# Steps of five engines issued in the order of a written timetable, in place of a list scheduler's order

## The chip, the cores and the metric

The kernel runs on one core of a Trainium2 chip. The metric is the device time of one execution in microseconds, the median of several runs. A core has five engines that work side by side: TensorE (PE, matmuls; PEld is its weight load), VectorE (DVE), ScalarE (ACT), GpSimd (POOL) and SyncE (SP, which here issues DMA transfers). Each takes its instructions strictly in the order in which the program wrote them; semaphores make an instruction wait for its inputs and for its buffer.

## The reference, cut to what matters

Two parts follow each other. The first is a gated recurrence with a complex decay for 4 batches, 8 heads, 768 time steps and 48 channels per head:

```python
mag = np.sqrt(a_re * a_re + a_im * a_im)
scale = np.minimum(mag, 0.999) / (mag + 1e-06)
a_re_n, a_im_n = (a_re * scale, a_im * scale)
for t in range(S):
    new_re = ar * S_re - ai * S_im
    new_im = ar * S_im + ai * S_re
    S_re, S_im = (new_re + kv, new_im)            # kv = outer(k[t], v[t])
    y[:, :, t] = einsum('bhd,bhde->bhe', q[:, :, t], S_re)
```

The second takes y as 3072 tokens of 384 features: `(sigmoid(x @ w_gate) * (x @ w_val)) @ w_out`, with 1536 hidden features. The result is 3072 x 384 in float32.

## The kernel before

**Slabs and groups.** The 768 time steps of a batch are cut into 6 chunks of 128, which gives 24 slabs of 128 tokens by 384 features (8 heads of 48). Slabs are taken in groups, `SIZES = [2, 3, 3, 3, 3, 3, 3, 3, 1]`. In logarithms the product of decays is a running sum, so a chunk becomes a masked attention (scores between q and k, each scaled by its decay and turned by its angle) plus a state that goes from chunk to chunk.

**The steps.** The program is a list of small steps, each on one engine, named by kind and slab m (or group g):

- *Loads, on SP:* `consts` (six constants), `la` (a_re and a_im of a slab), `lq` (k, q and v of a slab). The weights `wg`, `wv`, `wo` are loaded from POOL's queue in nine parts.
- *Phase A, for a whole group:* `sq` (squares, ACT, line 333); `add` and `min` on POOL (342, 350) make the capped squared size; `lna`, `lnm`, `inv` on ACT (358, 365, 371) take logarithms and a reciprocal; `r` on POOL (382) is the ratio of the parts; `cl` on PE (389) sums the logarithms over time; `ee` on ACT (396, 398) gives the decays as exp of plus and minus half the sum. `scr` and `rbe` on SP (405, 413) send the last row of the decays to DRAM and bring it back as columns.
- *Phase B:* `atan` on ACT (449).
- *Phase C, for each slab:* `ct` on PE (463, and 466 for what was carried from earlier chunks) sums the angles, `run` on POOL (479, 482) carries them on, `r16` on DVE (490) and `nid` on PE (498) take off whole turns, `cs` on ACT (506 to 509) takes cosine and sine. `v16` on POOL (433) casts v, `qke` on POOL (441) multiplies q and k by the decays, `ks` and `qs` on DVE (518) turn them.
- *Attention of a slab:* `tp` (PE, 548 and 549: 16 transposes in two halves), `qkT` (DVE, 556), `sc` (PE, 564), `mst` (DVE, 571: mask), `u` (DVE, 585 and 588: the state, decayed), `x16` (POOL, 598), `kv` (PE, 608), `P` (DVE, 618, 621: the new state), `y` (PE, 634, 636), `y16` (ACT, 646), `xp` (PE, 655), `xt` (DVE, 662).
- *The second part, for a group:* for each of 12 blocks of 128 hidden features, `pg` and `pv` (PE, 679, three matmuls each over all tokens of the group), `tanh` (ACT, 694), `p` (DVE, 701, the product); then for each slab `po` (PE, 717, 12 matmuls in three steps), `ot` (ACT, 727) and `st` (SP, 734, the store).

**Tables of ACT.** Phase A, B and C each need another table of functions (`SETS`); tanh is in those of B and C. Changing it is an instruction of its own (line 769, or the line of the instruction for which the compiler had to add it).

**Buffers.** Each tile kind has a fixed number of buffers: two for `a2` (the group's a), one for `sq`, six for q and k, four for v, and in PSUM four tiles for attention (`gen`) and four for the second part (`moe`).

**What sets the order.** `Plan.order` is a list scheduler. Each step has an engine, a cost, a due time and a list of steps that it must follow. The scheduler keeps a clock for each engine, takes the earliest start that any ready step could have, and picks, on that engine, the step with the earliest due time:

```python
t, _, k, eng = min((c for c in cand if c[3] == best[1]
                    and c[0] <= best[0] + SLACK),
                   key=lambda c: (c[1], c[0]))
```

Due times come from `RATE` (9.21 us a slab) and leads and lags (`LEAD`, `MOE_LAG`). A phase of the next group is entered by the rules in `may_enter`. The order found is written out once; the tile framework adds the semaphore waits.

Of the kernel before, what the change touches and what calls it, by code (L numbers as in the profile page):

```python
# [26 lines left out]
SIZES = [2, 3, 3, 3, 3, 3, 3, 3, 1]  # L27
RATE = 9.21
LEAD = {'la': 87.6, 'lq': -0.9, 'p0': 39.8, 'pa': 40.0, 'pb': 17.2}
MOE_LAG = -5.7  # L30
WGV_DUE, WOU_DUE, WGV_AFTER = -41.6, 45.5, 0
SLACK = 0.05
TAIL = {"pe": 0.21, "dve": 0.14, "act": 0.17, "pool": 0.11, "sp": 0.0}


class Plan:
# [6 lines left out]

    def __init__(self):
        self.steps, self.bufs, self.caps = {}, {}, {}

    def buf(self, name, tag, make):
        self.bufs[name] = [tag, make, 0]

    def add(self, key, eng, cost, due, emit, after=(), new=(), use=(),  # L50
            phase=None, load=0.0):
        for n in (*new, *use):
            self.bufs[n][2] += 1
        self.steps[key] = (eng, cost, due, emit, tuple(after), tuple(new),
                           (*new, *use), phase, load)

    def order(self, phases, may_enter):
        steps, bufs = self.steps, self.bufs
        users, waits = {}, {}
        for key, st in steps.items():  # L60
            waits[key] = len(st[4])
            for d in st[4]:
                users.setdefault(d, []).append(key)
        left = {n: b[2] for n, b in bufs.items()}
        freed = dict.fromkeys(bufs, 0.0)
        taken = {t: [] for t in self.caps}
        free = dict.fromkeys(ENGINES, 0.0)
        dma = 0.0
        done, placed, avail = {}, [], {}
        ready = {k for k in steps if not waits[k]}  # L70
        for k in ready:
            avail[k] = 0.0
        ph = 0
        while ready:
            while ph + 1 < len(phases) and may_enter(
                    phases[ph + 1], done, free["act"]):
                ph += 1
                if phases[ph][1]:
                    free["act"] += 1.3
            best = None  # L80
            cand = []
            for k in ready:
                eng, _, due, _, _, new, _, want, _ = steps[k]
                if want is not None and phases[ph][0] not in want:
                    continue
                t = max(avail[k], free[eng])
                for n in new:
                    tag = bufs[n][0]
                    old = taken[tag]
                    if len(old) >= self.caps[tag]:  # L90
                        m = old[-self.caps[tag]]
                        if left[m]:
                            t = None
                            break
                        t = max(t, freed[m])
                if t is None:
                    continue
                cand.append((t, due, k, eng))
                if best is None or t < best[0]:
                    best = t, eng  # L100
            if best is None:
                why = []
                for k in ready:
                    eng, _, due, _, _, new, _, want, _ = steps[k]
                    why.append((k, "phase" if want is not None and phases[ph][0] not in want else [ (n, taken[bufs[n][0]][-self.caps[bufs[n][0]]], ) for n in new if len(taken[bufs[n][0]]) >= self.caps[bufs[n][0]] and left[taken[bufs[n][0]][-self.caps[bufs[n][0]]]]]))
                raise RuntimeError(f"no step can be placed: {why} {phases[ph]}")
            t, _, k, eng = min((c for c in cand if c[3] == best[1]
                                and c[0] <= best[0] + SLACK),
                               key=lambda c: (c[1], c[0]))
            _, cost, _, _, _, new, uses, _, load = steps[k]  # L110
            ready.discard(k)
            free[eng] = t + cost
            end = t + cost + TAIL[eng]
            if load:
                dma = max(dma, t + cost) + load
                end = dma + 2.0
            for n in new:
                taken[bufs[n][0]].append(n)
            for n in uses:
                left[n] -= 1  # L120
                freed[n] = max(freed[n], end)
            done[k] = end
            placed.append(k)
            for u in users.get(k, ()):
                waits[u] -= 1
                avail[u] = max(avail.get(u, 0.0), end)
                if not waits[u]:
                    ready.add(u)
        assert len(placed) == len(steps), (len(placed), len(steps))
        self.length = max(done.values())  # L130
        return placed

    def emit(self, order):
        tiles = {}
        for key in order:
            st = self.steps[key]
            for n in st[5]:
                tiles[n] = self.bufs[n][1](n)
            st[3](tiles)


def act_us(n):
    return 0.06 + n * 0.00083


def dve_us(n, fast=False):
    return 0.065 + n / (1920.0 if fast else 960.0)


def pool_us(n, two=False):  # L150
    return 0.15 + n * 0.00215 if two else 0.05 + n * 0.0012


def pe_us(n, passes=1):
    return max(0.025, passes * n / 2400.0 + 0.002)
# [3 lines left out]
def kernel(  # L159
# [12 lines left out]
    nc = tc.nc  # L172
# [11 lines left out]
    NG = len(SIZES)  # L184
    NSLOT = 6
# [4 lines left out]
    nid_d = nc.inline_tensor(-eye, name="glk_nid")  # L190
    wl_d = nc.inline_tensor((tri - 0.5).astype(np.float32), name="glk_wl")
    wt_d = nc.inline_tensor((tri / TWO_PI).astype(np.float32), name="glk_wt")
    on_d = nc.inline_tensor(
        np.full((L, L), 1.0 / TWO_PI, np.float32), name="glk_on")
    msk_d = nc.inline_tensor(tri.astype(np.float32), name="glk_msk")

    def pool(name, bufs, **kw):
        return ctx.enter_context(tc.tile_pool(name=name, bufs=bufs, **kw))

# [6 lines left out]
    def kind(tag, bufs, shape, dt, where=work):  # L206
        plan.caps[tag] = bufs

        def declare(*ids, shape=shape, dt=dt):
            first = ids if isinstance(ids[0], str) else (tag, *ids)  # L210
            name = "_".join(map(str, first))
            plan.buf(name, tag, lambda name: where.tile(
                shape, dt, name=name, tag=tag, bufs=bufs))
            return name

        return declare
# [23 lines left out]
    plan.caps["slot"] = NSLOT  # L240

    def cload(shape, dt, src, name):
        t = const.tile(shape, dt, name=name)
        consts.append((t, src))
        return t

    consts = []
    wl_t = cload([L, L], F32, wl_d, "wl_t")
    wt_t = cload([L, L], F32, wt_d, "wt_t")
    on_t = cload([L, L], F32, on_d, "on_t")  # L250
    idn_t = cload([L, L], F16, idn_d, "idn_t")
    nid_t = cload([L, L], F16, nid_d, "nid_t")
    msk_t = cload([L, L], F32, msk_d, "msk_t")
# [18 lines left out]

    def heads(ap):
        return ap.rearrange("p (h d) -> p h d", d=D)

    def add(key, eng, cost, due, emit, **kw):
        plan.add(key, eng, cost, due, emit, **kw)
        return key


    def e_consts(T):
        for t, src in consts:
            nc.sync.dma_start(t, src.ap())

    add("consts", "sp", 2.7, -90.0, e_consts, load=1.8)
    gv_keys, ou_keys = [], []
    for i, f in enumerate(range(0, DFF, 512)):
        for nm, dst, src in (("wg", wg16, moe_w_gate), ("wv", wv16, moe_w_val)):
            def e(T, dst=dst, src=src, f=f):
# [4 lines left out]
            after = gv_keys[-1:] or [("min", WGV_AFTER)]  # L294
            gv_keys.append(add((nm, i), "pool", 0.77, WGV_DUE, e,
                               after=after, load=2.2))
    for i, j in enumerate(range(0, NFB, 4)):
        def e(T, j=j):
# [5 lines left out]
        ou_keys.append(add(("wo", i), "pool", 0.77, WOU_DUE, e,  # L304
                           after=(ou_keys or gv_keys)[-1:], load=2.2))
# [6 lines left out]
    last_run, last_P = {}, {}  # L312
    TANH_IN = [(x, g) for x in "BC" for g in range(NG)]
    for g, n in enumerate(SIZES):
        m0 = FIRST[g]
        at0 = m0 * RATE
        A, SQ, LM = t_a2(g), t_sq(g), t_lm(g)
        XT, PT = t_xt(g), t_p(g)
        phA, phB, phC = ("A", g), ("B", g), ("C", g)
        for s in range(n):  # L320
# [3 lines left out]
            def e(T, A=A, s=s, b=b, c=c):  # L324
                dma_in(T[A][:, 0, s], a_re, b, c)
                dma_in(T[A][:, 1, s], a_im, b, c)

            add(("la", m), "sp", 0.95, at0 - LEAD["la"] + s, e,
                after=[("la", m - 1)] if m else [],
                new=[A] if s == 0 else [], use=[A] if s else [], load=2.3)  # L330

        def e(T, A=A, SQ=SQ, n=n):
            nc.scalar.activation(out=T[SQ][:, :, :n], in_=T[A][:, :, :n],  # L333
                                 func=FT.Square)

        add(("sq", g), "act", act_us(2 * n * HD), at0 - LEAD["p0"], e,
            after=[("la", m0 + n - 1)], new=[SQ], use=[A])
        for s in range(n):
            m = m0 + s

            def e(T, SQ=SQ, LM=LM, s=s):
                nc.gpsimd.tensor_tensor(out=T[LM][:, s], in0=T[SQ][:, 0, s],  # L342
                                        in1=T[SQ][:, 1, s], op=ALU.add)
# [397 lines left out]
    for g in range(NG):  # L741
        if g:
            phases.append((("A", g), True))
# [57 lines left out]
```

## Time and profile before

| | |
|---|---|
| median of 3 runs | 331.49 us (330.77 to 332.27) |
| the profiled execution | 330.96 us |
| its span, first to last instruction | 328.5 us |
| mean granted clock of TensorE | 0.963 |
| busy: PE, DVE, ACT, POOL | 262.5, 206.5, 211.9, 166.1 us |
| table loads on ACT | 33 of 1.283 us |
| data moved by DMA | 32.68 MB, of that 3.54 from POOL's queue (weights) |

Busy times of an engine are the time in which at least one of its instructions runs. Matmuls are pipelined: each takes longer from start to end than the next one waits to start, so distances between starts tell what PE can do. A row of the timeline or chain gives start, duration, engine, line and tiles; "x4" says how many instructions were merged. A bracket at the end tells how long the engine stood idle before it and what released it. Group rows give busy time in total, the mean of one in ns, and then the idle time ahead. PEclk is the granted clock of TensorE as a share of full speed.

### The profile page before, as it was taken

The numbers are of one execution on the slowest core, as the hardware profiler recorded it, in microseconds if no ns is written. First come the engines' busy times: TensorE is split into PE (matmuls) and PEld (weight loads), VectorE is DVE, ScalarE is ACT, GpSimd is POOL, SyncE is SP. The second block draws the span as 40 slices with busy tenths as digits, with TensorE's granted clock in tenths as the row PEclk, the third lists the DMA queues.
The fourth block names the chain that finished last, engine by engine and source line by source line (L and its number), as shares of the span: only waits on it lengthen the run. The fifth ranks groups of instructions, "written<-read, shape, count | busy, mean of one in ns | idle before, by whom it ended". The sixth has DMA issues, their size and how long they took to land.

```text
span 328.5 us, 6196 instructions
## 1 busy us (share of the span) xinstructions
PE 262.5 (80%) x2256; PEld 169.7 (52%) x2256; DVE 206.5 (63%) x373; ACT 211.9 (65%) x354; POOL 166.1 (51%) x177
## 2 busy tenths in 40 slices
PE   0035685857978799898969989989999898999995
PEld 0012552535545455465646555656666565666564
DVE  2002930399699679287755696689567949891522
ACT  0356438666877987896389848867995358543433
POOL 0187275867997877687117961945485104000000
PEclk9997757799999999999998999999999999999999
DMA  6998995997999588581886048736120011002011
GB/s 124 188 182 128 189 178 85 138 196 108 160 123 218 76 129 160 123 145 11 148 166 113 1 82 154 153 54 118 50 26 2 0 50 28 0 2 73 2 48 48
DMA packets 152381, 32.68 MB, mean 99 GB/s; under 512 B 144904, under 2 KB 152352, under 8 KB 152352
## 3 DMA queue, kind: packets, MB, share of 16 engines
q1 hardware_dynamic: 148368, 28.76, 51.2%
q0 software_dynamic: 3984, 3.54, 7.6%
q8 instruction: 17, 0.28, 0.4%
q14 instruction: 12, 0.10, 0.1%
HBM read 31.07 MB, written 4.76 MB: 109 GB/s over the span
## 4 chain that ended last, share of the span: by engine, by line
PE 42%; ACT 20%; DVE 18%; issue 8%; SPq 4%; DMA 4%; POOL 3%; DVEq 0%; ACTq 0%; POOLq 0%
PE o L717 12%; PE g L679 8%; PE v L679 7%; PE cl L389 5%; ACT L769 5%; DVE qkT L556 4%; DVE p L701 3%; DVE qst L518 3%; DVE kst L518 3%; SPq L309 3%; PE ct L463 2%; ACT g L694 2%; ACT sq L333 2%; ACT a L449 2%; POOL lm L342 2%
## 5 line engine op out<-in xcount | busy, mean ns | idle before, releaser
L694 ACT ACTIVATE g<-g 128x384 f16<-128x384 f32 (+2 forms) x108 | 48.2, 456 | 55.4 <-PE g L679 53.5
L701 DVE SCALAR_TENSOR_TENSOR p<-g,v 128x384 f16<-128x384 f16 (+2 forms) x108 | 53.7, 504 | 23.2 <-PE v L679 15.7
L679 PE MATMUL g<-xt,wg 128*128 128x384 f16 (+2 forms) x324 | 65.5, 312 | 3.0 <-DVE xt L662 1.5
L679 PE MATMUL v<-xt,wv 128*128 128x384 f16 (+2 forms) x324 | 65.5, 312 | 0.9 <-DVE p L701 0.9
L717 PE MATMUL o<-wo,p 128*128 128x384 f16 x288 | 52.0, 326 | 0.0
L389 PE MATMUL cl<-lm,wl_t 128*128 128x384 f32 x48 | 22.7, 607 | 27.8 <-ACT lm L365 24.9
L441 POOL TENSOR_TENSOR qk<-qk,ee 128x768 f32<-128x768 f32 x24 | 43.3, 1813 | 2.0 <-ACT ee L398 2.0
L490 DVE TENSOR_SCALAR r<-ct 128x384 f16<-128x384 f32 x24 | 13.2, 552 | 43.9 <-PE ct L463 25.9
L679 PEld LDWEIGHTS <-wg 128*128 128x128 f16 x324 | 29.5, 99 | 20.5 <-issue 8.0
L679 PEld LDWEIGHTS <-wv 128*128 128x128 f16 x324 | 28.7, 99 | 17.0 <-issue 5.8
L518 DVE TENSOR_TENSOR kst<-qk,cs 128x768 f16<-128x768 f32 x24 | 26.1, 1089 | 17.6 <-ACT cs L509 17.5
L556 DVE COPY qkT<-tp 128x1024 f16<-128x1024 f16 x48 | 32.6, 683 | 6.9 <-PE tp L549 6.6
L598 POOL CAST x<-u 128x384 f16<-128x384 f32 x20 | 14.1, 707 | 44.4 <-DVE u L588 38.4
L717 PEld LDWEIGHTS <-p 128*128 128x128 f16 x288 | 27.1, 98 | 18.2 <-issue 2.1
L571 DVE TENSOR_TENSOR mst<-sc,msk_t 128x512 f16<-128x512 f32 x48 | 32.6, 684 | 5.5 <-PE sc L564 5.4
L342 POOL TENSOR_TENSOR lm<-sq 128x384 f32<-128x384 f32 x24 | 28.1, 1170 | 13.7 <-ACT sq L333 12.3
L769 ACT ACT_TABLE_LOAD x27 | 34.6, 1283 | 0.5
L382 POOL TENSOR_TENSOR a<-a 128x384 f32<-128x384 f32 x24 | 23.6, 1008 | 22.0 <-ACT a L371 19.5
L463 PE MATMUL ct<-a,wt_t 128*128 128x384 f32 x48 | 22.1, 544 | 8.9 <-ACT a L449 8.9
L549 PE MATMUL tp<-idn_t,qst 128*128 128x128 f16 x192 | 26.5, 221 | 3.2 <-DVE qst L518 3.2
L389 PEld LDWEIGHTS cl<-lm,wl_t 128*128 128x128 f32 x48 | 10.4, 235 | 34.9 <-ACT lm L365 28.9
L548 PE MATMUL tp<-idn_t,kst 128*128 128x128 f16 x192 | 27.0, 221 | 0.8 <-DVE P L618 0.4
(52 smaller groups left out, 462.6 us busy)
## 6 DMA issues: line engine op xcount, KB each, us to landing
a<-in_a_re_dram SPq DMA_DIRECT2D x24, 192.0 KB, 3.9
a<-in_a_im_dram SPq DMA_DIRECT2D x24, 192.0 KB
qk<-in_k_dram SPq DMA_DIRECT2D x24, 192.0 KB, 4.9
qk<-in_q_dram SPq DMA_DIRECT2D x24, 192.0 KB, 4.8
v<-in_v_dram SPq DMA_DIRECT2D x24, 192.0 KB, 4.1
out_dram<-ot SPq DMA_DIRECT2D x24, 192.0 KB, 1.9
wg<-in_moe_w_gate_dram POOLq DMA_DIRECT2D x3, 384.0 KB, 5.7
wv<-in_moe_w_val_dram POOLq DMA_DIRECT2D x3, 384.0 KB, 6.4
```

The source lines that it names most:

```text
L342: nc.gpsimd.tensor_tensor(out=T[LM][:, s], in0=T[SQ][:, 0, s], in1=T[SQ][:, 1, s], op=ALU.add)
L389: nc.tensor.matmul(T[CL][:, :HD], wl_t, T[LM][:, s], start=True, stop=True)
L441: nc.gpsimd.tensor_tensor(out=T[QK], in0=T[QK], in1=T[EE], op=ALU.mult)
L463: nc.tensor.matmul(ct, wt_t, T[A][:, 1, s], start=True, stop=False, skip_group_check=True)
L518: nc.vector.tensor_tensor(out=T[SL][i].rearrange("p h (r x) -> p h r x", r=2)[:, :, :, 0:D], in0=heads(T[QK][:, i]).unsqueeze(2) .broadcas ...
L556: nc.vector.tensor_copy(out=T[QT], in_=T[TP])
L571: nc.vector.tensor_tensor(out=T[MS], in0=T[SC], in1=msk_t.unsqueeze(1).broadcast_to([L, 4, L]), op=ALU.mult)
L679: nc.tensor.matmul(T[ACC][:, :nt], w[:, j, fb * 128:fb * 128 + 128], T[XT][:, j, :nt], start=(j == 0), stop=(j == 2))
L694: nc.scalar.activation(out=T[G16][:, :nt], in_=T[PG][:, :nt], func=FT.Tanh, scale=0.5)
L701: nc.vector.scalar_tensor_tensor(out=T[PT][:, fb, :nt], in0=T[G16][:, :nt], scalar=1.0, op0=ALU.add, in1=T[PV][:, :nt], op1=ALU.mult)
L717: nc.tensor.matmul(T[PO][:, :DM], T[PT][:, fb, s * L:(s + 1) * L], wo16[:, fb], start=(fb == 0), stop=(fb == NFB - 1))
L769: nc.scalar.preload_act_table_set(SETS[held])
```

## The change

The list scheduler, its costs, due times and phase rules go. In their place stands `TIMES`, a table with one time for each step (1,446 of them, by kind and in the order of slabs or groups) and for each of 29 table loads. `Plan.order` sorts all steps by that time and asserts that each follows the steps it depends on. The times do nothing else: no instruction waits for a time, and each engine gets its steps in sorted order. The semaphore waits are made as before.

Beside that: (1) the groups are 1, 2, 2, 2, 3, 3, 3, 3, 3 and 2 slabs; (2) `add`, `min`, `r` and `qke` of group 0 run on VectorE (`BRISK = 1`); (3) ACT's first table is loaded ahead of everything, and the other table loads are entries of the timetable; (4) the constants go out in two parts, behind the first `la` (0.7, 1.6, 2.95 and so on); (5) the first weight part follows the first `la` in place of `min` of slab 0; (6) the `rbe` transfers of neighbouring slabs of one batch in one group are one pair, issued when the last of them has its `scr`.

What the timetable lists, in its own us, by group:

| group | slabs | last la | sq | first cl | atan | last y | first pg | last p | last po |
|---|---|---|---|---|---|---|---|---|---|
| 0 | 0 | 0.7 | 5.0 | 7.5 | 11.4 | 23.4 | 28.6 | 56.7 | 65.9 |
| 1 | 1-2 | 11.4 | 16.5 | 24.2 | 30.9 | 56.2 | 58.3 | 79.4 | 82.8 |
| 2 | 3-4 | 30.2 | 38.1 | 44.6 | 51.1 | 75.2 | 85.8 | 104.2 | 110.4 |
| 3 | 5-6 | 49.4 | 55.7 | 62.0 | 65.6 | 91.7 | 106.3 | 127.6 | 135.1 |
| 4 | 7-9 | 67.8 | 73.6 | 83.4 | 88.8 | 117.8 | 128.6 | 157.4 | 174.8 |
| 5 | 10-12 | 87.5 | 94.1 | 106.6 | 112.4 | 151.8 | 157.9 | 187.3 | 197.6 |
| 6 | 13-15 | 109.8 | 116.4 | 129.7 | 136.8 | 179.9 | 187.8 | 217.3 | 235.2 |
| 7 | 16-18 | 135.6 | 140.2 | 159.0 | 164.7 | 211.0 | 216.6 | 245.8 | 257.0 |
| 8 | 19-21 | 160.9 | 168.4 | 188.3 | 195.4 | 236.3 | 245.9 | 266.8 | 276.4 |
| 9 | 22-23 | 199.9 | 212.2 | 218.2 | 221.8 | 245.5 | 266.8 | 284.2 | 287.5 |

The core of the diff:

```diff
-SIZES = [2, 3, 3, 3, 3, 3, 3, 3, 1]
-RATE = 9.21
...
+BRISK = 1
+SIZES = [1, 2, 2, 2, 3, 3, 3, 3, 3, 2]
+TIMES = {
+    "consts": [
+        1.6, 5.95],
+    "wg": [
+        9.61, 19.75, 36.31],
+    "wv": [
+        14.45, 28.31, 41.72],
+    "wo": [
+        47.02, 54.23, 60.97],
...
+    "table": [
+        10.565, 13.045, 17.81, 29.88, 34.29, 42.91, 49.12, 52.94, 59.64,
...
+    def order(self, times):
...
+        for kind, keys in kinds.items():
+            assert len(keys) == len(times[kind]), kind
+            at.update(zip(keys, times[kind]))
+        for i, t in enumerate(times["table"]):
+            at["table", "BCA"[i % 3]] = at.get(("table", "BCA"[i % 3]), ()) + (t,)
...
+        order = [key for _, _, key in sorted(rows)]
...
+    nc.scalar.preload_act_table_set(SETS["A"])
+    consts = [[], []]
...
+    def eng(g):
+        return nc.vector if g < BRISK else nc.gpsimd
...
-            after = gv_keys[-1:] or [("min", WGV_AFTER)]
+            after = gv_keys[-1:] or [("la", 0)]
...
-                nc.gpsimd.tensor_tensor(out=T[LM][:, s], in0=T[SQ][:, 0, s],
+                eng(g).tensor_tensor(out=T[LM][:, s], in0=T[SQ][:, 0, s],
...
-                            rbe[b][p0:p0 + D, c],
-                            scr[b][c].rearrange("(h d) -> d h", d=D))
+                            rbe[b][p0:p0 + D, lo:hi],
+                            scr[b][lo:hi].rearrange("c (h d) -> d c h", d=D))
...
+    order = plan.order(TIMES)
...
+            if key[0] == "table":
+                nc.scalar.preload_act_table_set(SETS[key[1]])
+                continue
```

`eng(g)` stands in the same way in `min`, `r` and `qke`.

482 lines of the change are left out of this document (215 added, 267 removed), and 154 rows, old and new, of the table TIMES.

## The prediction

> **What bounds the kernel now.** I read the page first, then the windows by stage, then the chain that ended last, and last the timeline of PE where the windows look thin. The page:
>
> ```profile
> span 328.5 us, 6196 instructions
> PE 262.5 (80%) x2256; PEld 169.7 (52%) x2256; DVE 206.5 (63%) x373; ACT 211.9 (65%) x354; POOL 166.1 (51%) x177
> ```
>
> The profiled execution took 330.96 us, 0.53 below the median of 331.49; its span is 328.5, so 2.5 us lie around it. The sum below is made against 330.96. PE is the busiest engine, but 80% busy is an upper view: the busy time counts the pipelined end of each matmul. What PE has to do is found from the distance between starts. First the y matmuls, then gate and value:
>
> ```profile
> 149.57 0.19 PE L634 MATMUL y<-x,qkT 128*128 128x48 f16 x1
> ...
> 149.95 0.18 PE L636 MATMUL y<-v,mst 128*128 128x48 f16 x1
> ```
>
> ```profile
> 311.10 0.65 PE L679 MATMUL v<-xt,wv 128*128 128x384 f16 x3
> 311.58 0.65 PE L679 MATMUL g<-xt,wg 128*128 128x384 f16 x3
> ```
>
> Sixteen y matmuls (eight on each of the two lines) start within 0.38 us, 0.025 each; three 384-column f16 matmuls of a gate step take 0.47 to the next step, and so does a value step. The chain has the others:
>
> ```profile
> 44.12 0.80 PE g L679 x3
> ...
> 135.60 1.29 PE cl L389 x4
> ...
> 160.32 4.55 PE o L717 x28
> ...
> 198.87 4.55 PE o L717 x28
> ...
> 295.00 4.55 PE o L717 x28
> ...
> 323.11 1.96 PE o L717 x12
> ```
>
> Here (the first row apart, the first gate step of all) 28 output matmuls take 4.55 us (0.1625 each) and four f32 matmuls of cl 1.29 (0.32 each). A slab, counted from the code, then needs: gate and value 72 pieces of 128 columns, 24 x 0.1625 = 3.90; output 12 x 0.1625 = 1.95; cl 2 and ct 2 or 4 (3.67 in the mean), 5.67 x 0.3225 = 1.83; the -1 matmul 0.16; 16 transposes, 8 scores and 3 output transposes of 128 columns, a third of 384, 27 x 0.054 = 1.46; kv and y, 21.3 x 0.025 = 0.54. That is 9.84 us, and 24 slabs need 236 us of PE at full clock. So 92 of the 328.5 us are PE doing nothing or going slowly. Where, by stage:
>
> ```profile
> core 0: us, PE busy (x) PEld busy (x) DVE busy (x) ACT busy (x) POOL busy (x), PEclk, DMA share, GB/s
> 0.00:20.00 20.00, 0.00 (x0) 0.00 (x0) 1.77 (x13) 5.73 (x5) 4.82 (x14) 1.00 1.09 161
> 20.00:44.00 24.00, 14.52 (x106) 8.64 (x107) 11.90 (x20) 11.74 (x17) 14.11 (x18) 0.80 1.10 165
> 44.00:60.00 16.00, 10.39 (x38) 6.45 (x38) 1.33 (x4) 12.06 (x18) 9.17 (x11) 0.71 0.80 134
> 60.00:80.00 20.00, 14.00 (x132) 9.42 (x131) 17.05 (x29) 11.61 (x21) 16.39 (x18) 0.96 1.08 154
> ...
> 220.00:240.00 20.00, 19.71 (x160) 12.78 (x159) 14.84 (x27) 16.57 (x29) 10.06 (x12) 1.00 0.33 70
> ```
>
> No matmul in the first 20 us; a thin, slow PE to 60 (granted clock 0.80, then 0.71); 14.0 of 20 us busy to 80, though at 0.96; nearly full at 220 to 240. So the time is lost early. In the chain the same work comes round every group: the output runs of 28 at 160.32, 198.87 and 295.00 stand at the same place of groups 2, 3 and 6. From 198.87 to 295.00 nine slabs take 96.13 us, 10.68 per slab, PE full for 9.84 / 10.68 = 0.92 of it. From 160.32 to 198.87 it is 12.85 per slab (0.77). Eight slabs had been through at 160.32; at the late pace they would have taken 85. How an order wastes PE early is seen at 48 to 55 us:
>
> ```profile
> 48.60 0.49 PE L679 MATMUL g<-xt,wg 128*128 128x256 f16 x3
> 51.48 3.83 PE L389 MATMUL cl<-lm,wl_t 128*128 128x384 f32 x6 [2.39 <-ACT lm L365]
> 55.14 0.49 PE L679 MATMUL v<-xt,wv 128*128 128x256 f16 x3
> ```
>
> Gate 5 of group 0 was done, value 5 stood behind cl of group 1 in PE's queue, and cl waited 2.39 us for ACT: 6.5 us between a gate matmul and its value, at low clock.
>
> **The change, part by part.**
>
> *The order and the group sizes.* The timetable gives an order only; nothing waits for a time. It has 1,446 step times and 29 table loads. Its groups of 1, 2, 2, 2 slabs bring the first gate matmul to 28.65 us in the list; the trace had it at 44.12, the first row of the chain's rows above. Counting the steps listed before 60: 5 cl 3.2, ct of slabs 0 to 4 5.8, 5 of nid 0.8, 7 halves of transposes 3.0 and 6 of scores 1.3, y, kv and xp 2.3, 24 gate and value steps of one slab 3.9 and 3 of two slabs 1.0: 21.3 us of PE work at the prices above. From 60 to 250 it lists 183 us in 190, PE full for 0.97. So the order claims the early stage, and a pace that before reached only in its best window.
>
> *Can the head be on time?* What before shows of it:
>
> ```profile
> 3.49 0.51 SPq L309 DMA_DIRECT2D a<-in_a_re_dram  x1
> ...
> 13.15 1.28 ACT L333 ACT_TABLE_LOAD   x1 [13.15 <-DMA a<-in_a_im_dram]
> ...
> 15.95 1.28 ACT L769 ACT_TABLE_LOAD   x1
> ...
> 21.08 2.92 PE L389 MATMUL cl<-lm,wl_t 128*128 128x384 f32 x4 [21.08 <-ACT lm L365]
> ```
>
> Slab 0's a came with slab 1's, behind six constants, and ACT then spent 1.28 on an implicit table load and 1.28 on the next. Now a of slab 0 is the first issue, the constants follow in two parts, and table A is loaded before any data: 2.8 us of SP (3.49 to 0.7) and one load of 1.28 go. But the loads still have to come: to feed the list up to its first output steps (60.8 to 65.9) 8 slabs of a, 6 of q, k and v, all nine weight parts and the constants, 16 x 0.197 + 18 x 0.197 + 9 x 0.393 + 0.32 = 10.5 MB, must move. At the 163 GB/s of the first two windows that is 64 us: no slack. Between 0 and 6 us late, I take 3. The list already holds the slow clock (the four cl matmuls at 21.08 took 2.92, twice the 1.29 above; it spaces the first group's gate and value at 0.54 where 0.17 would do at full clock).
>
> *The pace after 60.* 236.2 - 21.3 = 214.9 us of PE work are left. Bounds: 0.97 (the list) gives 221.5; 0.77 (the stage at 160) gives 279. Between them I take 9.84 / 10.68, what this chip did with the same tiles, buffers and engines over nine slabs under the old order: 233.2 us. The list is denser, but what it cannot hold is the disturbance of DVE and POOL (below), and a queue in fixed order passes lateness on.
>
> *Group 0's add, min, r and qke on VectorE.* The prices:
>
> ```profile
> L441 POOL TENSOR_TENSOR qk<-qk,ee 128x768 f32<-128x768 f32 x24 | 43.3, 1813 | 2.0 <-ACT ee L398 2.0
> ...
> L769 ACT ACT_TABLE_LOAD x27 | 34.6, 1283 | 0.5
> ...
> L342 POOL TENSOR_TENSOR lm<-sq 128x384 f32<-128x384 f32 x24 | 28.1, 1170 | 13.7 <-ACT sq L333 12.3
> ...
> L518 DVE TENSOR_TENSOR kst<-qk,cs 128x768 f16<-128x768 f32 x24 | 26.1, 1089 | 17.6 <-ACT cs L509 17.5
> L518 DVE TENSOR_TENSOR qst<-qk,cs 128x768 f16<-128x768 f32 x24 | 25.1, 1045 | 0.0
> L382 POOL TENSOR_TENSOR a<-a 128x384 f32<-128x384 f32 x24 | 23.6, 1008 | 22.0 <-ACT a L371 19.5 <-DMA qk<-in_k_dram 2.3
> ...
> L350 POOL TENSOR_SCALAR lm<-lm 128x384 f32<-128x384 f32 x24 | 16.2, 676 | 2.0
> L433 POOL TENSOR_SCALAR v<-v 128x384 f16<-128x384 f32 x24 | 15.7, 654 | 23.1 <-DMA v<-in_v_dram 12.4 <-PE y L636 9.0
> ...
> L598 POOL CAST x<-u 128x384 f16<-128x384 f32 x20 | 14.1, 707 | 44.4 <-DVE u L588 38.4 <-PE v L679 5.8
> ...
> L694 ACT ACT_TABLE_LOAD x5 | 6.4, 1283 | 0.1
> ```
>
> POOL loses 1.17 + 0.68 + 1.01 + 1.81 = 4.7 us of work; DVE gains four instructions, by kst (1.09 for 768 columns, half for 384) about 0.55 x 3 + 1.09 = 2.7, when it has 1.77 us of work in 20. Slab 0 gets through 2 us earlier; behind it PE waits for the loads of slabs 1 and 2, so I put 0 on the end (bounds -2 and 0).
>
> *Table loads* fall from 33 (27 + 5 + 1) to 30: 3.9 us of ACT. A tenth group adds five group instructions and 12 tanh and 12 products. ACT lists at most 14.5 us in 15 (105 to 120), mostly less; the cover is PE, which is fuller. 0, with +2 if the cover goes. *36 more matmuls each of gate and value* have the same columns: 72 x 0.005 = 0.4 us, in the density.
>
> *rbe merged by group and batch:* 48 issues become 26, one with up to three columns of 384 elements:
>
> ```profile
> rbe<-scr SPq DMA_DIRECT2D x48, 1.5 KB, 2.2
> ```
>
> A column landed 2.2 us behind its issue. u of a group's first slab now waits for the last slab's ee, scr and the larger transfer; u stands in DVE's queue ahead of products and kst, which would wait with it. The list has u 3.4 us or more behind rbe, below 5 in four groups. Landing as before, the wait is covered; three times as long, 6.6, each of the four stalls DVE some 2.5 us. Bounds 0 and 10; I take 0, the nearest row. The weights now go out behind the first load instead of behind min of slab 0: in the 64 us above.
>
> *The end.* The chain's last output matmuls finish at 325.07 and the span at 328.5: copy, store and landing 3.4 us, as before.
>
> **Sum:** 60 + 3 + 233.2 + 3.4 + 2.5 = 302.1, against 330.96 (331.5 by the median).
>
> **Contention, rule against row.** qke on POOL beside DVE:
>
> ```profile
> 63.24 1.83 POOL L441 TENSOR_TENSOR qk<-qk,ee 128x768 f32<-128x768 f32 x1
> ...
> 64.66 2.19 DVE L518 TENSOR_TENSOR kst<-qk,cs 128x768 f16<-128x768 f32 x1 [1.06 <-ACT cs L509]
> ```
>
> ```profile
> 99.89 0.95 DVE L518 TENSOR_TENSOR kst<-qk,cs 128x768 f16<-128x768 f32 x1
> ...
> 101.28 0.51 POOL L350 TENSOR_SCALAR lm<-lm 128x384 f32<-128x384 f32 x1
> ```
>
> kst took 2.19 us while qke was running on POOL, and 0.95 elsewhere; min takes 0.68 in the mean and 0.51 in the row shown. The Trainium skill ("SBUF — State Buffer", section "Who interferes with whom") says that a VectorE instruction with two SBUF inputs and a GpSimd instruction that reads SBUF share a port pair that one holds for its whole length, so that the other is fully blocked. The trace agrees in kind (2.19 is 0.95 plus 1.24, and qke ran to 65.07); by it the sum would be the second rival's, if every such block lay on PE's path.
>
> **The rivals.**
>
> *The list is met.* PE at 0.97, head on time: 60 + 221.5 + 3.4 + 2.5 = 287.4. For it: the list spaces output steps at 0.65, as the rows have them, and the last stretch of before ran gate and value back to back (the rows at 311). Against: the early slices, and three engines listed nearly full at once.
>
> *DVE and POOL block each other on PE's path.* Mean less undisturbed: kst 0.14 and qst 0.10 (against 0.95), add 0.16 (against r, which has its shape), min 0.17, v 0.14 and x 0.20 (against 0.51): 0.91 us a slab, some 20 slabs after 60, 18 us on top of the met list with the late head: 287.4 + 3 + 18 = 308. Against: much of it falls where PE has other work.
>
> *Only the start gains.* The order keeps nothing of its density: the first gate matmul comes 15.5 us sooner (44.12 to 28.65), 331 - 15.5 = 315.5, and one slab in hand instead of two takes back up to half a slab, 4.9: 316 to 320. It then does not do what it says.
>
> *PE stays at the slow clock* (the side slower than before). The place is 60 us on. Each us of PE work at half clock costs another, so 29 of the 214.9 at half clock, a clock of 0.5 up to about 120 us, eats the whole gain; 35 would give 337. For it: 0.71 in 44 to 60. Against: 0.96 in 60 to 80 and 1.00 behind, with a thinner PE than the list has.
>
> **How the numbers follow.** Base case 0.52 (its own range 292 to 308: density 0.95 to 0.91, head 0 to 6 late); the met list 0.18; blocking 0.16; start only 0.06; slow clock or another stall of over 2.1 us a slab 0.06; and 0.02 for no change within 0.5% (1.7 us, about what a measurement here can tell). The predicted time is the base case's, 302. The range 287 to 315 takes in the met list and the blocking case and leaves out some 0.14. Faster 0.91, same 0.02, slower 0.07.
>
> **What would show it.** Right: first gate matmul near 29 us, PE's windows from 60 on at 18.5 of 20 or more, output runs some 10.5 us a slab apart, clock 1.00 from 65, loads at 160 GB/s to 60. Wrong: PE idle behind tp or ct with releaser DVE or ACT each group (blocking); u waiting for rbe; SP's queue held by stores while ACT waits for a; rows of cl at 0.64 apart after 70 us (slow clock).

## The result and the profile after

| | before | after |
|---|---|---|
| median | 331.13 us (4 runs, 329.80 to 332.27) | 301.45 us (4 runs, 300.27 to 302.56) |
| ratio after / before | | 0.910, 95% interval 0.905 to 0.916 |
| the profiled execution, and its span | 330.96, 328.5 us | 302.56, 300.8 us |
| mean granted clock | 0.963 | 0.977 |

The changed kernel is faster by 29.7 us, within 1 us of the forecast. The head, a term of the forecast's sum, was 5.4 us longer than forecast, the pace behind it 4.1 us shorter, and the tail 0.8 us shorter, so the errors nearly cancel. First the page of the changed kernel, its span and the busy time of each engine:

```profile
span 300.8 us, 6265 instructions
PE 258.9 (86%) x2328; PEld 177.2 (59%) x2328; DVE 212.2 (71%) x389; ACT 208.9 (69%) x368; POOL 161.9 (54%) x173
```

The busy times hardly moved (PE 262.5 to 258.9, DVE 206.5 to 212.2); the span around them shrank. The windows by stage, with the same columns as before (length, busy time and instructions of PE, PEld, DVE, ACT and POOL, granted clock, DMA share, GB/s), tell where:

```profile
0.00:20.00 20.00, 5.79 (x22) 2.79 (x23) 7.19 (x21) 9.83 (x14) 2.81 (x11) 1.00 0.97 163
20.00:44.00 24.00, 12.84 (x91) 8.12 (x91) 7.81 (x15) 16.30 (x28) 18.66 (x21) 0.97 1.07 157
44.00:60.00 16.00, 13.04 (x138) 9.58 (x137) 14.48 (x25) 12.18 (x22) 10.89 (x12) 0.83 1.07 163
60.00:80.00 20.00, 15.34 (x130) 10.71 (x129) 16.84 (x26) 13.05 (x24) 13.41 (x15) 0.83 0.82 142
80.00:100.00 20.00, 18.52 (x200) 13.87 (x196) 14.45 (x28) 16.93 (x31) 12.12 (x14) 1.00 0.75 125
100.00:120.00 20.00, 18.33 (x172) 13.36 (x171) 17.49 (x36) 17.38 (x30) 14.64 (x15) 1.00 1.14 180
120.00:140.00 20.00, 19.57 (x216) 15.05 (x215) 16.70 (x32) 17.14 (x35) 18.51 (x19) 1.00 0.66 116
...
220.00:240.00 20.00, 19.77 (x210) 13.71 (x209) 19.00 (x34) 17.33 (x31) 8.44 (x10) 1.00 0.00 1
```

PE works from the first window on (5.79 us busy in 20, where it had none), the loads keep moving 157 to 163 GB/s to 60 us, and from 80 us on the PE windows are at 18.3 or more of 20. One window is thin: 60 to 80, with 15.34 busy and a clock of 0.83. The forecast's signs had windows of 18.5 from 60 on and a clock of 1.00 from 65; neither came yet in this window. A finer window shows where the clock was low:

```profile
63.20:70.00 6.80, 5.77 (x39) 4.21 (x39) 5.25 (x9) 5.13 (x8) 2.07 (x3) 0.50 1.26 202
```

The timeline of PE just ahead of it and in it, with start, duration and, in brackets, how long PE stood idle before the row and what released it:

```profile
58.85 0.18 PE L794 MATMUL y<-v,mst 128*128 128x48 f16 x1
63.67 0.48 PE L659 MATMUL ct<-r,nid_t 128*128 128x384 f16 x1 [4.63 <-DVE r L652]
```

PE waited 4.63 us for `r16` on VectorE. The timeline of VectorE at that place shows what `r16` (L652) stood behind:

```profile
57.30 0.68 DVE L729 TENSOR_TENSOR mst<-sc,msk_t 128x512 f16<-128x512 f32 x1
57.90 4.28 DVE L743 TENSOR_TENSOR arr<-rbe 128x8 f32<-128x8 f32 x1
62.28 0.87 DVE L746 TENSOR_TENSOR u<-P,arr 128x384 f32<-128x384 f32 x1
63.07 0.54 DVE L652 TENSOR_SCALAR r<-ct 128x384 f16<-128x384 f32 x1
```

`arr`, the product of two decay columns of 8 elements ahead of the state update `u`, took 4.28 us. The summary of that tile (count, least / median / greatest duration in ns) says 0.16 is normal:

```profile
L743 DVE TENSOR_TENSOR arr<-rbe x20: 151/160/4280, 45.0 to 256.5; 128x8 f32<-128x8 f32 x20
```

And GpSimd's timeline in the same microseconds:

```profile
57.48 1.83 POOL L606 TENSOR_TENSOR qk<-qk,ee 128x768 f32<-128x768 f32 x1
59.26 0.99 POOL L640 TENSOR_TENSOR run<-run,a 128x384 f32<-128x384 f32 x1
60.21 1.93 POOL L514 TENSOR_TENSOR lm<-sq 128x384 f32<-128x384 f32 x2
62.23 1.28 POOL L522 TENSOR_SCALAR lm<-lm 128x384 f32<-128x384 f32 x2
```

Four instructions (the third row holds two) follow one another with no gap, the next recorded as starting before the last has ended; the first gap is at 60.21 + 1.93 = 62.14, and `arr` ends at 62.18.

### The profile page after: what moved, and what is told of

The parts are those of the page before. It is cut to its first block, busy times and chain, and to the rows that moved or that the text cites. A ratio compares the mean times of both kernels' runs of the same rounds, so it can differ in the third digit from the quotient of the medians.

```text
span 300.8 us, 6265 instructions
## 1 busy us (share of the span) xinstructions
PE 258.9 (86%) x2328; PEld 177.2 (59%) x2328; DVE 212.2 (71%) x389; ACT 208.9 (69%) x368; POOL 161.9 (54%) x173
## 4 chain that ended last, share of the span: by engine, by line
PE 38%; DVE 15%; POOL 14%; issue 10%; ACT 7%; SPq 7%; DMA 7%; DVEq 0%; POOLq 0%; ACTq 0%
PE o L862 10%; PE v L832 8%; PE g L832 8%; SPq L473 4%; POOL lm L514 4%; POOL lm L522 4%; PE cl L556 4%; DVE arr L743 3%; DVE p L848 3%; POOL qk L606 2%; DMA rbe<-scr 2%; DMA a<-in_a_re_dram 2%; DVE mst L729 2%; PE sc L722 2%; DVE kst L676 2%
## 5 line engine op out<-in xcount | busy, mean ns | idle before, releaser
L832 PE MATMUL g<-xt,wg 128*128 128x384 f16 (+2 forms) x360 | 67.7, 298 | 5.0 <-ACT g L842 4.4
L832 PE MATMUL v<-xt,wv 128*128 128x384 f16 (+2 forms) x360 | 67.8, 298 | 0.3 <-DVE p L848 0.2
L862 PE MATMUL o<-wo,p 128*128 128x384 f16 x288 | 56.5, 328 | 0.0
L832 PEld LDWEIGHTS <-wg 128*128 128x128 f16 x360 | 32.3, 99 | 20.4 <-issue 10.0
L832 PEld LDWEIGHTS <-wv 128*128 128x128 f16 x360 | 32.8, 100 | 15.8 <-issue 4.7
L550 POOL TENSOR_TENSOR a<-a 128x384 f32<-128x384 f32 x23 | 25.8, 1143 | 30.2 <-ACT a L540 25.1
L514 POOL TENSOR_TENSOR lm<-sq 128x384 f32<-128x384 f32 x23 | 24.9, 1094 | 25.6 <-ACT sq L506 25.3
L862 PEld LDWEIGHTS <-p 128*128 128x128 f16 x288 | 27.4, 98 | 16.7 <-issue 1.7
L676 DVE TENSOR_TENSOR qst<-qk,cs 128x768 f16<-128x768 f32 x24 | 23.9, 997 | 0.0
L705 PEld LDWEIGHTS <-kst 128*128 128x128 f16 x192 | 19.7, 103 | 6.7 <-DVE kst L676 4.3
L706 PEld LDWEIGHTS <-qst 128*128 128x128 f16 x192 | 19.6, 103 | 5.6 <-DVE qst L676 2.7
```

The lines of the kernel that those rows point to most:

```text
L514: eng(g).tensor_tensor(out=T[LM][:, s], in0=T[SQ][:, 0, s], in1=T[SQ][:, 1, s], op=ALU.add)
L676: nc.vector.tensor_tensor(out=T[SL][i].rearrange("p h (r x) -> p h r x", r=2)[:, :, :, 0:D], in0=heads(T[QK][:, i]).unsqueeze(2) .broadcas ...
L705: nc.tensor.transpose(tp[:, 4 + i], ks[:, h], idn_t)
L706: nc.tensor.transpose(tp[:, i], qs[:, h], idn_t)
L832: nc.tensor.matmul(T[ACC][:, :nt], w[:, j, fb * 128:fb * 128 + 128], T[XT][:, j, :nt], start=(j == 0), stop=(j == 2))
L862: nc.tensor.matmul(T[PO][:, :DM], T[PT][:, fb, s * L:(s + 1) * L], wo16[:, fb], start=(fb == 0), stop=(fb == NFB - 1))
```

## The experiments

The fifth -1 matmul (`nid` of slab 4, L659, the row at 63.67 above) serves below as the mark where the head ends, and the last of the 24 (at 244.6) as the mark where the evenly paced part ends.

**1. Is it the written order, or what came with it?** Two kernels keep the list scheduler: one has only the new sizes, the other every edit but the timetable.

```diff
-SIZES = [2, 3, 3, 3, 3, 3, 3, 3, 1]
+SIZES = [1, 2, 2, 2, 3, 3, 3, 3, 3, 2]
```

> The kernel before with the group sizes 1, 2, 2, 2, 3, 3, 3, 3, 3, 2 alone, list scheduler. Theory 'order': 320 to 336 us, since ten groups cost three more table loads on ScalarE and the scheduler's leads are as before. Rival 'sizes': 305 to 318 us, first gate matmul near 30 us.

> The kernel before with every edit of the change except the timetable: new group sizes, group 0's sums on VectorE, first table ahead, constants in two parts, weights behind the first load, merged rbe; the order is the list scheduler's, with its old leads. Theory 'the written order makes the gain': 318 to 334 us, PE still thin from 44 to 100 us. Rival 'the smaller first groups and the earlier head make it': 300 to 312 us.

Measured: sizes alone 339.38 us, ratio 1.029 (1.023 to 1.035); all but the order 338.39, ratio 1.026 (1.020 to 1.033). Both are slower than the kernel before, so the theory's figures (up to 334 and 336) were too low as well. The windows of the second one:

```profile
44.00:60.00 16.00, 11.65 (x115) 8.91 (x116) 11.64 (x22) 12.31 (x20) 11.77 (x13) 0.79 0.78 125
60.00:80.00 20.00, 15.14 (x171) 10.93 (x169) 15.02 (x31) 15.44 (x29) 17.53 (x20) 1.00 0.93 148
80.00:100.00 20.00, 14.33 (x160) 10.86 (x159) 13.86 (x27) 10.17 (x19) 6.97 (x11) 0.91 1.04 172
100.00:120.00 20.00, 16.55 (x88) 10.12 (x86) 4.79 (x12) 18.38 (x28) 13.61 (x14) 0.91 0.66 96
```

Its PE also starts early (4.83 us busy in the first 20), but runs at 14.33 and 16.55 of 20 where the timetable has 18.52 and 18.33. The order alone is worth 338.39 - 301.45 = 37 us; the rest of the change, under the old scheduler, costs 8. The scheduler kept the leads and lags that belonged to the old groups. A list scheduler with leads set anew for the new groups was not run, so the 37 us hold against this list scheduler and not against any.

**2. Group 0 on VectorE.** `BRISK = 0` puts its four sums back on GpSimd.

> The changed kernel with group 0's add, min, r and qke back on GpSimd, at the same places of the timetable. Theory 'loads set the head': 300 to 303 us, slab 0 some 2 us later and the first group's gate matmuls behind it, nothing later on. Rival 'the head is tight and passes lateness on': 303 to 306 us.

Measured: 301.44 us, ratio 0.916 (0.912 to 0.919). No difference, as the forecast's term said: the first gate matmul stands at 30.57 in this kernel and at 31.12 in the changed one. What was expected of the first steps held in part: slab 0's -1 matmul comes 1.8 us later (16.30 against 14.47), but the gate matmuls behind it do not.

**3. What holds `arr` up: its data or GpSimd?** `arr` reads a constant tile of zeros in place of the decays that come back from DRAM, so the state carried from chunk to chunk drops out of the result.

```diff
+    one = const.tile([128, NCH, H], F32, name="one")
+    nc.vector.memset(one, 0.0)
...
-                        out=arr[b][:, c], in0=rbe[b][:, c - 1],
-                        in1=rbe[b][:, c], op=ALU.mult)
+                        out=arr[b][:, c], in0=one[:, c - 1],
+                        in1=one[:, c], op=ALU.mult)
```

> The changed kernel with the product of decay columns (arr) taken from a constant tile of zeros in place of rbe: the carried state drops out of the result, arr has the same shape and two SBUF inputs, and waits for no transfer. Theory 'GpSimd holds the port pair while it runs four instructions in a row': arr near 58 us still takes 3 to 4.5 us, time 300 to 303. Rival 'arr waits for the rbe transfer in a full DMA queue': arr takes 0.16 us, PE comes out of the head 4 us sooner, 296 to 298 us.

Measured: 301.26 us, ratio 0.915 (0.911 to 0.919). VectorE's timeline of this kernel:

```profile
57.43 4.29 DVE L745 TENSOR_TENSOR arr<-one 128x8 f32<-128x8 f32 x1
```

The same stall with no transfer to wait for. The data are out. Next, GpSimd's queue gets a gap there: `x16` of slab 3, which needs `u` and so waits for VectorE, moves from 61.74 to 55.6 in the table, between `qke` of slab 3 and `run` of slab 4. (The expectation calls these slabs groups.)

```diff
-        44.56, 52.75, 61.74, 66.95, 77.85, 102.23, 111.15, 116.88,
+        44.56, 52.75, 55.6, 66.95, 77.85, 102.23, 111.15, 116.88,
```

> The changed kernel with one time of its table altered: the step x16 of group 3 (time 61.74) gets 55.6, so that it stands in GpSimd's queue between qke (group 3) and run, not behind them. It needs u of group 3 from VectorE, so GpSimd must stop and wait there. Theory A (VectorE's arr of group 3, 4.28 us in the changed kernel, is shut out as long as GpSimd runs one instruction right after another: 1.83 + 0.99 + 1.93 us): arr now ends with the one GpSimd instruction that it meets, so it measures at most 1.9 us, nid of group 4 on TensorE (L659 at 63.67 in the changed kernel) comes 2 to 3 us sooner, and the time is 2 to 3 us under 301.4, i.e. 298 to 300, ratio to before about 0.905. Rival B (arr is long for a reason of its own, in its data): arr stays over 4 us, and since GpSimd now waits for it, run and add come later: 302 to 306.

Measured: 298.34 us, ratio 0.904 (0.901 to 0.908); its six runs (297.01 to 299.82) lie below all four of the changed kernel. VectorE's and GpSimd's timelines of this kernel:

```profile
56.58 1.40 DVE L743 TENSOR_TENSOR arr<-rbe 128x8 f32<-128x8 f32 x1
...
58.56 0.55 DVE L652 TENSOR_SCALAR r<-ct 128x384 f16<-128x384 f32 x1
```

```profile
56.11 1.84 POOL L606 TENSOR_TENSOR qk<-qk,ee 128x768 f32<-128x768 f32 x1
58.71 0.50 POOL L756 CAST x<-u 128x384 f16<-128x384 f32 x1 [0.76 <-DVE u L746]
```

`qke` ends at 57.95, GpSimd then waits, and `arr` ends at 57.98. The fifth -1 matmul moves from 63.67 to 59.17, and PE's wait in front of it falls from 4.63 to 1.50:

```profile
59.17 0.32 PE L659 MATMUL ct<-r,nid_t 128*128 128x384 f16 x1 [1.50 <-DVE r L652]
```

Of the 4.5 us these 3.1 are what the broken row gave. The other 1.4 came ahead of it, since the fourth -1 matmul already stands at 55.21 here and at 56.57 in the changed kernel; the edit does not explain them. The same way out by taking instructions out of the row: the sums of groups 0 to 2 on VectorE.

```diff
-BRISK = 1
+BRISK = 3
```

> The changed kernel with the sums of groups 0, 1 and 2 on VectorE, where the changed kernel has group 0's alone; same table. Theory A (GpSimd's unbroken row of instructions near 57 to 62 us makes arr last 4.28 us): GpSimd is less behind there, arr shrinks to under 2 us and the start of the full pace comes 2 to 4 us sooner: 297 to 300. Rival B (VectorE is the engine short of time in the first 60 us: two more groups of add, min, r and qke there put some 3 us on it for each group): nid of group 4 comes 0 to 4 us later than 63.7 and the time is 301 to 306.

Measured: 297.83 us, ratio 0.904 (0.900 to 0.908). The summary of `arr` in this kernel, where none is longer than 0.89 us, and the one that had taken 4.28 takes 0.15:

```profile
L743 DVE TENSOR_TENSOR arr<-rbe x20: 149/160/886, 45.8 to 252.3; 128x8 f32<-128x8 f32 x20
```

Of the row at 57 to 62 us only `qke` has left GpSimd, which then stands idle from 57.65 to 59.13; `arr` falls there, at 58.40. That GpSimd's unbroken row makes `arr` long is shown. Both kernels beat the changed one, with the same work and the same result: by some 3 us in the medians, and by 2 if the ratios are compared (0.904 against 0.910), since the kernel before, run beside these experiments, had medians of 329.84 to 330.79 and not 331.13.

**4. Does TensorE's own work set the pace behind the head?** The forecast's largest term, 233.2 us, was TensorE's work divided by a density. One kernel leaves work of TensorE out: the 40 matmuls that add what earlier chunks carried to the row sums of the angles (12.9 us). Another leaves out `min` on GpSimd from group 1 on, the cap of the squared size (17 us).

```diff
-                if prev:
-                    nc.tensor.matmul(ct, on_t, T[prev[0]], start=False,
-                                     stop=False, skip_group_check=True)
```

> The changed kernel without the carry matmuls of ct (the second matmul of each accumulating pair, 40 in all, so the on_t product is left out of the row sums); everything else stays. At 0.3225 us for one of them TensorE has 12.9 us less to do. Theory A (from 65 us on TensorE's own work sets the end): 8 to 13 us less, about 290. Rival B (the other engines or the steps' dependencies set the pace, and TensorE only looks full because it waits in instructions): 3 us less or under that, 298 to 302, with TensorE's windows of 20 us down by about 1 us each.

```diff
-                eng(g).tensor_scalar(
-                    out=T[LM][:, s], in0=T[LM][:, s], scalar1=CAP,
-                    scalar2=-1.0, op0=ALU.min, op1=ALU.max)
+                if g < BRISK:
+                    eng(g).tensor_scalar(
+                        out=T[LM][:, s], in0=T[LM][:, s], scalar1=CAP,
+                        scalar2=-1.0, op0=ALU.min, op1=ALU.max)
```

> The changed kernel without the min on GpSimd for the groups from 1 on (its input is used unclipped), about 17 us of GpSimd's 162. Theory A (TensorE's own work sets the end from 65 us on, GpSimd matters only in the head): what it gains is the head's lateness alone, 1 to 4 us: 297.5 to 300.5. Rival B (GpSimd holding VectorE up costs a little at every group): 5 us or more, 296 or under, with the gain spread over all windows, not in the first 65 us.

Measured: without the carry matmuls 299.95 us, ratio 0.910 (0.905 to 0.915); without `min` 296.0 us, ratio 0.897 (0.893 to 0.901). Leaving out 12.9 us of TensorE's work gained 1.5, and by the ratio nothing (0.910 both times). By the marks (table below) 0.8 of its gain lies behind the head, where 16 slabs have lost 32 x 0.3225 = 10.3 us of matmuls. Theory A fell there. What PE waits for in the kernel without carry, from 80 to 240 us (total, times, longest):

```profile
PE ct L656 <- DVE r L649: 4.7, 7, 1.5
PE y L789 <- POOL x L753: 1.7, 2, 1.4
PE tp L703 <- DVE qst L673: 1.4, 3, 0.5
```

In the changed kernel the first of these is 0.5 in the same stretch. Much of the freed time turned into waits, most of all for the next result of VectorE. Without `min` the head gained 3.9 us and the paced part 2.6 of the 12.8 us taken out there. The whole gain, 5.4 us, is rival B's size, but most of it is in the head, as theory A had it; so neither is borne out whole.

**5. Which engine can take more?** Four kernels, each with more to do on one engine, by repeating an instruction whose result stays the same. The added lines, one kernel after the other: three matmuls of `po` (PE), every second `p` (DVE), every second `tanh` (ACT), and `v16` (POOL):

```diff
+                    for fb in range(3 if i == 0 and 2 <= g <= 7 else 0):
+                        nc.tensor.matmul(
+                            T[PO][:, :DM], T[PT][:, fb, s * L:(s + 1) * L],
+                            wo16[:, fb], start=True, stop=True)
...
+                for _ in range(2 if 2 <= g <= 7 and fb % 2 == 0 else 1):
...
+                for _ in range(2 if 2 <= g <= 7 and fb % 2 == 0 else 1):
...
+                for _ in range(3 if 3 <= m <= 16 else 1):
```

> The changed kernel with the first three output matmuls (po) of each slab of groups 2 to 7 done twice: 48 more matmuls at 0.328 us = 15.7 us of TensorE's work between about 100 and 255 us; the result is the same. This run and the next three each give one engine some 16 us more to do in the same stretch. Theory A (TensorE's own work sets the pace from 65 us on): the whole of it, +14 to +17 us (315 to 318), while the same load on another engine costs 2 us or less. Theory B (no engine's work alone; each engine waits for the others in the order of the queues, and TensorE's empty time, 5.6 us between 80 and 240 us, can be used): +5 to +11 us, 306 to 312.

> The changed kernel with every second product p (gate by value) of groups 2 to 7 done twice on VectorE: 36 more instructions at 0.47 us = 16.9 us; the result is the same. Theory A (TensorE's work sets the pace; VectorE has 24 us idle in the 160 us from 80 to 240): +0 to +2 us. Theory B (coupled queues): +5 to +14 us, 306 to 315.

> The changed kernel with every second tanh of groups 2 to 7 done twice on ScalarE: 36 more instructions at 0.43 us = 15.4 us; the result is the same. Theory A (TensorE's work sets the pace): +0 to +2 us. Theory B (coupled queues): +4 to +12 us, 305 to 313.

> The changed kernel with the conversion of v to half precision (v16) of slabs 3 to 16 done three times on GpSimd: 28 more instructions at 0.59 us = 16.4 us; the result is the same. GpSimd has 48 us idle in the 160 us from 80 to 240, the most of the four. Theory A (TensorE's work sets the pace): +0 to +2 us. Theory B (coupled queues, and GpSimd holding VectorE up besides): +2 to +10 us, 303 to 311.

The expectations meant some 16 us for each engine, but TensorE got half of that. They took a matmul by its duration of 0.328 us, and matmuls overlap. In the kernel with more matmuls three added ones (L862) and the four behind them (L866) read:

```profile
115.07 0.65 PE L862 MATMUL o<-wo,p 128*128 128x384 f16 x3
115.56 0.81 PE L866 MATMUL o<-wo,p 128*128 128x384 f16 x4
```

Three matmuls push the next one back by 0.49 us, 0.163 each, the forecast's own price of 0.1625. So 48 are 7.8 us of work, not 15.7. On the other engines a repeat does cost about its duration: two `tanh` in a row take 0.80 us where one takes 0.38, two `p` 0.86 where one takes 0.41, and three `v16` 1.70.

The results, with the starts of the marks from the traces; the added work is what that line of the engine had more or less between the two marks, in instructions and us (matmuls by the distance between starts):

| kernel | median | ratio and interval | fifth nid | last nid | between | added there | cost there |
|---|---|---|---|---|---|---|---|
| changed | 301.45 | 0.910 (0.905-0.916) | 63.67 | 244.59 | 180.92 | | |
| x16 early | 298.34 | 0.904 (0.901-0.908) | 59.17 | 240.44 | 181.27 | 0 | +0.4 |
| groups 0-2 on DVE | 297.83 | 0.904 (0.900-0.908) | 59.73 | 240.37 | 180.64 | 0 | -0.3 |
| no carry (PE) | 299.95 | 0.910 (0.905-0.915) | 60.10 | 240.17 | 180.08 | -32 matmuls, -10.3 | -0.8 |
| no min (POOL) | 296.00 | 0.897 (0.893-0.901) | 59.78 | 238.09 | 178.31 | -17 min, -12.8 | -2.6 |
| PE + | 306.64 | 0.929 (0.925-0.933) | 63.15 | 247.21 | 184.06 | 36 matmuls, 5.9 | +3.1 |
| ACT + | 305.98 | 0.928 (0.923-0.933) | 60.98 | 247.61 | 186.63 | 32 tanh, 14.0 | +5.7 |
| DVE + | 316.73 | 0.956 (0.950-0.963) | 63.60 | 257.41 | 193.81 | 31 p, 15.5 | +12.9 |
| POOL + | 319.49 | 0.968 (0.963-0.973) | 62.23 | 260.42 | 198.20 | 26 v16, 17.0 | +17.3 |

One trace stands for each kernel. In two more kernels, group 0's sums on GpSimd and the constant `arr`, 180.89 and 180.11 us lie between the marks, so a difference of under 1 us there is not told from none; the kernel without carry is such a case.

ScalarE and TensorE, the busiest engine, took their additions best: 5.7 us of 14.0 show, and 3.1 of 5.9 (for TensorE 5.2 of 7.8 in the whole time). VectorE passed on 12.9 of 15.5, and GpSimd, the least busy, all of it. The times fit theory B's ranges for TensorE and ScalarE and lie above them for VectorE (316.73, at most 315 expected) and GpSimd (319.49, at most 311). Theory A falls by the last three, which it priced at 2 us or less each, and by the kernel without carry. The kernel with more matmuls alone decides little: at the right price theory A asks for up to 7.8 us, and 5.2 came. Its page shows PE's busy time up by 6.6 us, from 258.9, near the 7.8 and far from 15.7:

```profile
PE 265.5 (87%) x2376; PEld 181.3 (59%) x2376; DVE 210.4 (69%) x389; ACT 209.8 (69%) x368; POOL 161.5 (53%) x173
```

In the kernel with more on GpSimd not all of the 17.3 us need be waits. Its clock fell again behind the head, in three stretches, where the changed kernel has 1.00 from 80 us on:

```profile
108.60:112.00 3.40, 3.35 (x8) 1.81 (x9) 1.72 (x2) 0.77 (x2) 2.61 (x4) 0.52 0.96 197
153.00:156.40 3.40, 3.40 (x9) 1.69 (x8) 1.13 (x2) 3.15 (x6) 0.86 (x1) 0.52 0.02 5
180.30:187.10 6.80, 5.85 (x44) 3.65 (x44) 3.73 (x8) 2.77 (x5) 3.76 (x6) 0.51 0.68 114
```

PE was busy for 12.6 us in them at about half clock, so by estimate up to 6 us of the cost are the clock's. What set the clock back there was not tested. PE's waits from 80 to 240 us in the kernel with more on GpSimd show how a load there arrives at TensorE:

```profile
PE y L792 <- POOL x L756: 1.0, 1, 1.0
PE cl L556 <- ACT lm L535: 0.8, 2, 0.5
```

```profile
PE y L793 <- POOL x L757: 5.2, 2, 3.1
PE cl L556 <- ACT lm L535: 3.9, 2, 2.4
PE ct L628 <- POOL run L641: 2.4, 1, 2.4
```

The first fence is the changed kernel, the second the one with more on GpSimd: `y` behind `x16`, `ct` behind `run`, and `cl` behind a logarithm on ScalarE that takes GpSimd's `min` as its input. GpSimd's extra instructions stood, in a fixed queue, ahead of steps that others were due to use.

## Why the prediction was right, point by point

- **The order (302.1 of the sum; "only start gains" 316 to 320).** The order makes the gain: with the old scheduler the same sizes and tables are slower than before (experiment 1). The first gate matmul came at 31.12; the list has 28.65 and the forecast said near 29. The density was kept, so that rival is out.
- **Head, 60 + 3 (bounds 0 and 6): mis-sized.** The first output step is listed at 60.80 and stands at 69.17, so the head was 8.4 late, outside the bounds. The loads, on which the 3 and the bounds rested, were not the cause of most of it: they had been named as without slack, and they did move 157 to 163 GB/s. Of the 8.4, the wait behind the VectorE stall is 4.6 us, of which 3.1 go when one step of GpSimd is moved; 2.2 were there before it (that matmul is listed at 56.81 and stood at 63.67), and 1.5 came behind it, where the clock was 0.50 (63.2 to 70.0). The 2.2 were not traced to a cause. Nor were the 1.5: with `x16` early the same stretch, from the fifth -1 matmul to the first output step, took 6.5 us and not 5.5, though its clock was low for only half as long (62.2 to 65.6). The head had been costed by its transfers alone, with no term for VectorE and GpSimd in it.
- **Pace, 214.9 us of TensorE's work at 0.92 = 233.2: size off by 4.1, and its reason is not borne out.** From 68.4 (60 and 8.4) to 297.5, where the last copy to the store begins, are 229.1 us, 0.94 by the forecast's count. Together with the later head (5.4) and a tail of 3.3 and 1.8 around the span in place of 3.4 and 2.5, that makes 60 + 8.4 + 229.1 + 3.3 + 1.8 = 302.6. The number came out since the head's error and the pace's nearly cancel. As a mechanism, "TensorE's work at a density" is refuted for small changes: 10.3 us of it less gained 0.8, and of 5.9 more about half shows (3.1). That the density is the outcome of how the fixed queues interlock, and served as a size because the work on each engine was nearly the same before and after, is the reading that fits; no run shows it by itself.
- **"The list is met" (287.4).** Not met. Behind the head the timetable and the chip still drift apart: the last -1 matmul is listed at 228.64 and starts at 244.59, 16 late, of which 6.9 were there at the fifth one.
- **"DVE and POOL block each other on PE's path" (308).** The mechanism is there, and the one block that was traced to PE lies at a place the rival didn't name, in the head. What the shorter blocks behind it cost PE, which the rival put at 0.91 us a slab, was not measured apart. These are the summaries by line of the changed kernel (least / median / greatest ns):

```profile
L746 DVE TENSOR_TENSOR u<-P,arr x20: 557/558/1311, 45.3 to 256.8; 128x384 f32<-128x384 f32 x20
...
L676 DVE TENSOR_TENSOR kst<-qk,cs x24: 942/992/1644, 16.4 to 246.4; 128x768 f16<-128x768 f32 x24
L676 DVE TENSOR_TENSOR qst<-qk,cs x24: 941/951/1296, 17.3 to 251.4; 128x768 f16<-128x768 f32 x24
...
L652 DVE TENSOR_SCALAR r<-ct x24: 544/551/558, 13.9 to 243.7; 128x384 f16<-128x384 f32 x24
...
L775 DVE TENSOR_TENSOR P<-u,kv x16: 541/545/555, 52.0 to 255.4; 128x384 f32<-128x384 f32 x16
...
L729 DVE TENSOR_TENSOR mst<-sc,msk_t x48: 675/683/692, 20.6 to 260.9; 128x512 f16<-128x512 f32 x48
```

  `arr`, `u`, `kst` and `qst`, with both inputs in SBUF, are stretched, at most to 27, 2.3, 1.7 and 1.4 times their median; `r16`, `P` and `mst`, with an input from PSUM, stay within 17 ns. The Trainium skill ("SBUF — State Buffer", section "Who interferes with whom") names just this division; the trace agrees with it. The same page calls the pair an exclusive lock for the whole instruction, by which `arr` would wait for the one instruction of GpSimd that was running, here 1.83 us long; it waited for four.

  The forecast's own pair of rows fits this too, and was read too narrowly. `kst` ran from 64.66 to 66.85 in the kernel before, and `qke` covers only the first 0.41 us of that. The next step of GpSimd had followed it without a gap:

```profile
65.02 1.01 POOL L479 TENSOR_TENSOR run<-run,a 128x384 f32<-128x384 f32 x1
...
66.12 2.28 POOL L433 TENSOR_SCALAR v<-v 128x384 f16<-128x384 f32 x2
```

  The first gap is at 66.03, and `kst` lost 1.24 us over its 0.95, three times what `qke` alone had left.
- **Terms put at 0.** Group 0 on VectorE: 0 measured (301.44 with it undone). `rbe` merged: the forecast feared 10 us; `arr` with no transfer at all ran in 301.26, so nothing. Table loads: 30, as counted; ScalarE's cover was there in part, since 15.4 us more on it cost 4.5.
- **Slow clock (337).** 0.83 in the two windows from 44 to 80, with 0.50 from 63.2 to 70.0, and 1.00 behind; the clock did not eat the gain.

What stays open: which of the waits in the fixed queues binds the pace. More work costs most on GpSimd and VectorE, yet 12.8 us less on GpSimd in the paced part gave back only 2.6, so, by what was tried, no single engine is the bound in both directions. The price of an addition also depends on where it stands in its queue, and each was tried at one place only.

## What to carry to other kernels

An order written out for all queues can be the whole gain (37 us of 338 here), and the smaller groups that came with it lost time under the list scheduler. A busy share near full is no proof that an engine sets the pace: take some work off that engine and see whether the time follows, then add 5% to each engine in turn and see who passes it on. Price matmuls by the distance between their starts, not by their durations. Where queues are fixed, look for unbroken rows on GpSimd beside short VectorE instructions with two SBUF inputs, and put into such a row a step that has to wait for VectorE.

## What was not expected of the hardware

A VectorE instruction of 0.16 us was shut out for 4.28 us by four GpSimd instructions in a row, and got in at the first gap between two of them. In all nine kernels with the timetable in which that row was left alone, this `arr` took 3.42 to 4.29 us. With a wait put into the row it was 1.40; with those sums off GpSimd, none was over 0.89.
